# Gated linear attention with a max-out layer: a new opening, eight items transposed on TensorE, and three loads issued from ScalarE's queue

## The chip, the cores and the metric

The kernel runs on one core of a Trainium2 chip. The core has five engines with queues of their own: TensorE (PE in the profile; its weight loads are the row PEld), VectorE (DVE), ScalarE (ACT), GpSimd (POOL) and SyncE (SP), which here only issues transfers. Sixteen DMA engines move data between the device memory and the core. The metric is the device time of one execution in microseconds. The profile's span, from the first to the last instruction, is a little shorter than that time: 168.3 us of span stand beside 170.57 us for the profiled execution.

## What is computed

The inputs q, k, v and alpha have the shape 4 batches x 8 heads x 768 tokens x 48, in float32. A state of 48x48 for each batch and head decays and is updated token by token, and its product with q is the input of a max-out layer:

```
state = alpha[t][:, None] * state + outer(k[t], v[t])
y[t]  = q[t] @ state                      # for each batch and head
x     = y, heads side by side             # 3072 tokens x 384
h1    = x @ w1 ; h2 = x @ w2              # 384 x 1024 each
out   = maximum(h1, h2) @ w_out           # 1024 x 384
```

## The kernel before

**The attention.** The work is cut into 12 items: item n is one batch and 256 tokens of it, three items to a batch, laid out as 128 partitions with two tokens (index j) in each. Lines 403 to 685 (`attention(n)`) plan one item. ScalarE takes the logarithm of alpha (`ln`), VectorE adds pairs of it (`su`), and TensorE turns that into running sums with a triangular matrix (`cs`, lines 435 to 443). ScalarE takes two exponentials of the sums (`en`, `ep`) and one of the few decay factors (`gg`). GpSimd multiplies k by `en` (`kt`, line 474), VectorE multiplies q by `ep` (`qt`, line 480), GpSimd casts v (`vc`, line 489). Both products must be turned so that the head dimension lies on partitions. Items 0 to 4 (the tuple `TURN`, line 194) do it on TensorE against an identity matrix (line 510, 16 products an item) followed by two copies out of PSUM (`ck`, `cq`, line 338 on ScalarE or 340 on VectorE); items 5 to 11 do it by two DMA transposes (line 522). Then come the scores (`sc`, line 620), their mask (`pt`, line 628), the state (`kv`, line 540; `w`, `t32` and `T`, lines 575 to 600, the only chain from one item to the next) and the output `y` (line 674), which is cast into `xT` (`xe`).

**The max-out layer.** Since maximum(h1, h2) = relu(h1 - h2) + h2, the kernel computes relu(x @ (w1 - w2)) @ w_out + x @ (w2 @ w_out). The difference `wd16` (line 375) and the product `m16` (transposes at line 360, products at line 392) are made once from the weights. After that a `group` of tokens needs eight h products of three matmuls each (line 701), eight relus (709 on VectorE, 711 on ScalarE), and for every 128 tokens three matmuls with `m16` (726) and eight with `wo16` (728), an eviction and a store (736). The groups are 2, 3, 3, 3, 3, 3, 3, 2 and 2 blocks of 128 tokens wide.

**What sets the order.** The order on every engine is written out ahead of time. `Plan` (lines 29 to 165) is a list scheduler that runs when the program is built: every operation has estimated durations on the engines that may run it, dependencies, buffers and a priority (smaller first). `run` steps through an estimated clock, gives each idle engine the ready operation of the smallest priority, and emits the instructions in the order in which they started there. On the chip every engine takes its instructions in that fixed order; if an operand comes later than the estimate said, the engine waits, even where other work behind it would be ready. Attention has the priority 100 n plus a small number; the groups have 3000 and more, so they always come behind the attention. A load costs 1.31 us of the plan's transfer time, a DMA transpose 1.15 us. All transfers, transposes and stores are issued by SP, in one order: item 0, then w2, w1 and w_out in quarters (line 323), then items 1 to 11.

**The start.** GpSimd makes the constant matrices (`setup_pool1`) and then clears the pads of the v and T tiles (lines 262 and 276). VectorE derives others from them (`setup_dve1`, `setup_dve2`, lines 250 to 272), and item 0's `su` comes after these on VectorE.

Of the kernel before, what the change touches and what calls it, by code (L numbers as in the profile page):

```python
# [24 lines left out]
class Op:  # L25
    __slots__ = ("name", "engs", "emit", "deps", "takes", "uses", "prio", "mode", "xfer", "eng", "start", "end", "seen", "n")


class Plan:
# [4 lines left out]
    LEAD = 3.0  # L34

    def __init__(self, pools):
        self.free = dict(pools)
        self.banks = [True] * 8
        self.ops = []

    def room(self, takes):
        need = {}
        for b in takes:
            need[b.pool] = need.get(b.pool, 0) + 1
        for p, k in need.items():
            if p == "A":
                if self.pair() is None:
                    return False
            elif p == "M":
                if not any(self.banks):  # L50
                    return False
            elif self.free[p] < k:
                return False
        return True
# [7 lines left out]
    def take(self, b):  # L62
# [3 lines left out]
        elif b.pool == "M":  # L66
            free = [i for i in range(7, -1, -1) if self.banks[i]]
            half = [i for i in free if not self.banks[i ^ 1]]
            b.at = (half or free)[0]
            self.banks[b.at] = False  # L70
        else:
            self.free[b.pool] -= 1

    def give(self, b):
        if b.pool == "A":
            self.banks[b.at] = self.banks[b.at + 1] = True
        elif b.pool == "M":
            self.banks[b.at] = True
        else:
            self.free[b.pool] += 1  # L80

    def add(self, name, engs, emit, deps=(), takes=(), uses=(), prio=0.0, mode=None, xfer=0.0):
        o = Op()
        o.name, o.engs, o.emit, o.prio, o.mode, o.xfer = name, engs, emit, prio, mode, xfer
# [10 lines left out]
    def run(self):  # L95
        idle = {e: 0.0 for e in self.LAT}
        mode = None
        dma = 0.0
        order = []
# [3 lines left out]
        while waiting:  # L103
# [9 lines left out]
            for o in waiting:  # L113
# [6 lines left out]
                if ready is None:  # L120
# [6 lines left out]
                for e, dur in o.engs.items():  # L127
# [6 lines left out]
                    key = (o.prio, o.n)  # L134
                    if e not in best or key < best[e][0]:
                        best[e] = (key, o, dur)
            done = set()
            for e, (key, o, dur) in sorted(best.items(), key=lambda x: x[1][0]):
# [5 lines left out]
                if e == "PE" and o.mode != mode:  # L144
                    dur += self.SWITCH
                    mode = o.mode
# [3 lines left out]
                if e == "SP":  # L150
                    dma = max(dma, t + 1.3) + o.xfer
# [17 lines left out]
def kernel(  # L169
# [23 lines left out]
    WMAX = 384  # L193
    TURN = (0, 1, 2, 3, 4)
# [3 lines left out]
    NLD = 20  # L198
# [14 lines left out]
    plan = Plan({"ld": NLD, "en": 2, "loga": 2, "qk": 3, "pt": 4, "w": 4, "t32": 3, "gg": 3, "g": 2, "g16": 3, "outs": 6})  # L213
# [24 lines left out]
    def setup_pool1(eng):  # L238
        make_upper_triangular(nc, u16, val=1.0, diag=True)
        nc.gpsimd.memset(half1, 0.0)  # L240
# [7 lines left out]
        make_identity(nc, ident16)  # L248

    def setup_dve1(eng):  # L250
        nc.vector.memset(s16s[0][:, :, D:64], 0.0)
        nc.vector.memset(s16s[1][:, :, D:64], 0.0)
        nc.vector.tensor_sub(out=cmat, in0=u16, in1=half1)
        nc.vector.memset(cmat[0:64, 64:128], 0.0)
        nc.vector.tensor_sub(out=us16, in0=u16, in1=ident16)
        nc.vector.tensor_scalar_mul(out=nid16, in0=ident16, scalar1=-1.0)
        for i in range(2):
            nc.vector.memset(qkts[i].rearrange("p a j h d -> p (a j h) d")[:, :, D:64], 0.0)

    def setup_pool2(eng):  # L260
        for t in v16s:
            nc.gpsimd.memset(t.rearrange("p j h d -> p (j h) d")[:, :, D:96], 0.0)

    def setup_dve2(eng):
# [7 lines left out]
        nc.vector.memset(qkts[2].rearrange("p a j h d -> p (a j h) d")[:, :, D:64], 0.0)  # L272

    def setup_pool3(eng):
        for t in T16s:
            nc.gpsimd.memset(t, 0.0)

    s_p1 = plan.add("setp1", {"POOL": 2.6}, setup_pool1, prio=-100)
    s_d1 = plan.add("setd1", {"DVE": 2.6}, setup_dve1, deps=[s_p1], prio=-100)
    s_p2 = plan.add("setp2", {"POOL": 1.6}, setup_pool2, deps=[s_p1], prio=-90)  # L280
    s_d2 = plan.add("setd2", {"DVE": 1.3}, setup_dve2, deps=[s_d1], prio=-80)
    s_p3 = plan.add("setp3", {"POOL": 1.5}, setup_pool3, deps=[s_p2], prio=80)


    LX = 1024 * 20.5 / 16e3
    ld = {}

    def add_load(n, which, prio):
        src = {"a": alpha, "q": q, "k": k, "v": v}[which]
        b, c = divmod(n, NDB)  # L290
        buf = Buf("ld")

        def emit(eng):
            t = A["ld", n, which] = ldp.tile([128, H, 2 * D], FP32, tag="ld", name=which + "f")
            nc.sync.dma_start(  # L295
                out=t, in_=src[b, :, c * 256 : (c + 1) * 256, :].rearrange("h (p j) d -> p h (j d)", j=2)
            )

        ld[n, which] = (plan.add(f"ld{which}{n}", {"SP": 0.65}, emit, takes=[buf], prio=prio, xfer=LX), buf)

    WX = 384 * 1024 / 400e3
    wl = {}

    def add_wload(name, i, prio):
# [3 lines left out]
        def emit(eng):  # L308
            if name == "wo":
                t = ldp.tile([128, 2, DM], FP32, tag="ld", name="wof")  # L310
                nc.sync.dma_start(
                    out=t, in_=src[i * 256 : (i + 1) * 256, :].rearrange("(s p) d -> p s d", p=128)
                )
            else:
                t = ldp.tile([128, 3, 256], FP32, tag="ld", name=name + "f")
                nc.sync.dma_start(
                    out=t, in_=src.rearrange("(s p) f -> p s f", p=128)[:, :, i * 256 : (i + 1) * 256]
                )
            A["w", name, i] = t

        wl[name, i] = (plan.add(f"ld{name}{i}", {"SP": 0.5}, emit, takes=[buf], prio=prio, xfer=WX), buf)

    seq = [("d", 0)] + [("w2", i) for i in range(4)] + [("w1", i) for i in range(4)] + [("wo", i) for i in range(4)]
    seq += [("d", n) for n in range(1, ND)]
    pos = 0
    for name, i in seq:
        if name == "d":
            for w in "aqkv":
                add_load(i, w, -1000 + pos)
                pos += 1  # L330
        else:
            add_wload(name, i, -1000 + pos)
# [11 lines left out]
    w2c, wdc, woc, ptc = [], [], [], []  # L344
    for i in range(4):
        o, b = wl["w2", i]
        w2c.append(plan.add(
            f"w2c{i}", {"ACT": 0.83, "DVE": 0.55, "POOL": 1.25},
            lambda eng, i=i: cast(eng, w216[:, :, i * 256 : (i + 1) * 256], A["w", "w2", i]),
            deps=[o], uses=[b], prio=50 + i))  # L350

    for i in range(4):
        ps = Buf("M")

        def emit(eng, i=i, ps=ps):
            tp = A["wtp", i] = bank(ps, 384).bitcast(FP16).rearrange("p (u m) -> p u m", u=6)
            for u in range(2):
                for s in range(3):
                    f = 2 * i + u
                    nc.tensor.transpose(tp[:, 3 * u + s, :], w216[:, s, f * 128 : (f + 1) * 128], ident16)  # L360

        tr = plan.add(f"wtp{i}", {"PE": 0.34}, emit, deps=[w2c[i], s_p1], takes=[ps], prio=60 + i, mode=0)
        ptc.append(plan.add(
            f"wtc{i}", {"DVE": 0.6, "ACT": 0.8},
            lambda eng, i=i: cast(eng, w2T[:, 2 * i : 2 * i + 2, :].rearrange("p u m -> p (u m)"),
                                  A["wtp", i].rearrange("p u m -> p (u m)")),
            deps=[tr], uses=[ps], prio=61 + i))

    for i in range(4):
        o1, b1 = wl["w1", i]  # L370
        o2, b2 = wl["w2", i]

        def emit(eng, i=i):
            e = nc.vector if eng == "DVE" else nc.gpsimd
            e.tensor_sub(out=wd16[:, :, i * 256 : (i + 1) * 256], in0=A["w", "w1", i], in1=A["w", "w2", i])

        wdc.append(plan.add(f"wd{i}", {"DVE": 1.0, "POOL": 1.9}, emit, deps=[o1, o2], uses=[b1, b2], prio=70 + i))
    for i in range(4):
        o, b = wl["wo", i]
        woc.append(plan.add(  # L380
            f"woc{i}", {"ACT": 0.83, "DVE": 0.55, "POOL": 1.25},
            lambda eng, i=i: cast(eng, wo16[:, 2 * i : 2 * i + 2, :], A["w", "wo", i]),
            deps=[o], uses=[b], prio=74 + i))

    mc = []
    for s in range(3):
        ps = Buf("M")

        def emit(eng, s=s, ps=ps):
            mp = A["mp", s] = bank(ps, DM)  # L390
            for f in range(NF):
                nc.tensor.matmul(mp, lhsT=w2T[:, f, s * 128 : (s + 1) * 128], rhs=wo16[:, f, :],  # L392
                                 start=(f == 0), stop=(f == NF - 1))

        mm = plan.add(f"mp{s}", {"PE": 1.3}, emit, deps=ptc + woc, takes=[ps], prio=78 + s, mode=0)
        mc.append(plan.add(f"mc{s}", {"ACT": 0.48, "DVE": 0.5},
                           lambda eng, s=s: cast(eng, m16[:, s, :], A["mp", s]), deps=[mm], uses=[ps], prio=79 + s))
# [5 lines left out]
    def attention(n):  # L403
# [10 lines left out]
        loga_b = Buf("loga")  # L414

        def e_ln(eng):
            t = A["loga", n] = wk.tile([128, H, 2, D], FP16, tag="loga", name="loga")
# [367 lines left out]
```

## Time and profile before

| | |
|---|---|
| time, three runs | 171.43 us (169.94 to 171.87) |
| span of the profiled execution | 168.3 us |
| TensorE busy | 134.8 us (80%), 2144 matmuls |
| VectorE, ScalarE, GpSimd busy | 77.8, 84.1, 71.5 us |
| first matmul starts, last one ends | 8.47 us, about 164.9 us |
| read from and written to device memory | 23.59 and 4.72 MB |

The page gives the busy time of each engine, then the span in 40 slices of 4.2 us with one digit of busy share each, then the chain of work that ended last, and the groups of instructions by line. A busy TensorE is not a TensorE at its best: the ends of its matmuls are modelled, and at a lower clock the same matmuls are busy longer. So it takes two readings, how long it was idle and how long the same instruction took in different stretches.

### The profile page before, as it was taken

How to read it: one execution, taken by the hardware profiler on the slowest of the kernel's cores; microseconds unless marked ns; L12 is line 12 of the kernel's file. 1: busy time of each engine (PE TensorE's matmuls, PEld its weight loads, DVE VectorE, ACT ScalarE, POOL GpSimd, SP SyncE). 2: the span in 40 equal slices, each digit the busy share in tenths (PEclk: the TensorE clock that was granted, in tenths of full speed). 3: DMA queues.
4: the chain of work that ended last, by engine and by line, in shares of the span. 5: the costliest groups of instructions: out<-in, count | busy, mean ns of one | idle time of the engine just before them, and what ended most of it. 6: DMA issues, size and time to landing. Idle time of an engine off the chain costs nothing.

```text
span 168.3 us, 5032 instructions
## 1 busy us (share of the span) xinstructions
PE 134.8 (80%) x2144; PEld 89.6 (53%) x2144; DVE 77.8 (46%) x136; ACT 84.1 (50%) x155; POOL 71.5 (42%) x113
## 2 busy tenths in 40 slices
PE   0058599967884868969599894789989999999991
PEld 0047466745673645636256672545645666667660
DVE  3939922849678856618269564651930000001100
ACT  3255657453836549533563365262145482926342
POOL 7647900959794696781706467094100000000000
PEclk9999999999999699999879999699999999999999
DMA  5999999999999999999999999967210212103112
GB/s 142 265 346 348 370 280 238 274 247 266 310 241 277 251 257 247 197 268 246 200 237 208 235 254 219 263 78 156 90 51 0 93 47 76 68 25 117 47 47 93
DMA packets 72469, 32.29 MB, mean 192 GB/s; under 512 B 65280, under 2 KB 72448, under 8 KB 72448
## 3 DMA queue, kind: packets, MB, share of 16 engines
q1 hardware_dynamic: 72448, 31.99, 81.7%
q8 instruction: 16, 0.26, 0.7%
q14 instruction: 5, 0.04, 0.1%
HBM read 23.59 MB, written 4.72 MB: 168 GB/s over the span
## 4 chain that ended last, share of the span: by engine, by line
PE 49%; DMA 26%; DVE 7%; POOL 5%; SPq 4%; issue 4%; ACT 3%; DVEq 0%; ACTq 0%; POOLq 0%
PE PS L701 13%; PE PS L728 13%; DMA af<-in_alpha_dram 11%; DMA qk<-qkt 8%; PE PS L674 6%; PE PS L726 5%; DMA vf<-in_v_dram 4%; DMA w2f<-in_moe_w_dram 3%; PE PS L392 3%; SPq L295 3%; DVE pt L628 2%; PE PS L620 2%; POOL qkt L474 2%; PE PS L435 2%; PE PS L510 1%
## 5 line engine op out<-in xcount | busy, mean ns | idle before, releaser
L701 PE MATMUL PS<-xT,wd 128*128 128x384 f16 (+1 forms) x216 | 37.6, 319 | 3.9 <-ACT xT L338 2.6
L728 PE MATMUL PS<-wo,g 128*128 128x384 f16 x192 | 37.2, 326 | 0.0
L628 DVE TENSOR_TENSOR pt<-PS,mask 128x1024 f16<-128x1024 f32 x24 | 28.1, 1217 | 3.8 <-PE PS L620 3.5
L701 PEld LDWEIGHTS <-wd 128*128 128x128 f16 x216 | 20.3, 99 | 15.8 <-issue 4.7
L474 POOL TENSOR_TENSOR qkt<-kf,en 128x768 f16<-128x768 f32 x12 | 21.7, 1813 | 14.9 <-ACT gg L460 6.9
L711 ACT ACTIVATE g<-PS 128x384 f16<-128x384 f32 (+1 forms) x55 | 24.5, 458 | 6.3 <-PE PS L701 5.9
L709 DVE TENSOR_SCALAR g<-PS 128x384 f16<-128x384 f32 (+1 forms) x17 | 7.8, 493 | 37.8 <-PE PS L701 37.1
L338 ACT COPY outs<-PS 128x384 f32<-128x384 f32 x23 | 11.0, 478 | 28.2 <-PE PS L728 28.2
L728 PEld LDWEIGHTS <-g 128*128 128x128 f16 x192 | 18.1, 98 | 11.8 <-ACT g L711 0.2
L418 ACT ACTIVATE loga<-af 128x768 f16<-128x768 f32 x12 | 10.1, 843 | 18.8 <-DMA af<-in_alpha_dram 18.8
L620 PE MATMUL PS<-qk 48*64 48x128 f16 x384 | 9.5, 233 | 9.6 <-DMA qk<-qkt 5.1
L435 PE MATMUL PS<-s,cmat 128*128 128x384 f16 x24 | 8.4, 385 | 9.2 <-DVE s L425 8.5
L726 PE MATMUL PS<-m,xT 128*128 128x384 f16 x72 | 15.7, 326 | 0.0
L489 POOL CAST v<-vf 128x768 f16<-128x768 f32 x12 | 9.9, 823 | 13.0 <-DMA vf<-in_v_dram 12.8
L575 POOL TENSOR_TENSOR T<-w,gg 48x192 f16<-48x192 f32 x24 | 12.9, 539 | 4.3 <-DVE w L600 3.4
L620 PEld LDWEIGHTS <-qk 48*64 48x64 f16 x384 | 7.3, 115 | 13.1 <-issue 12.2
L480 DVE TENSOR_TENSOR qkt<-qf,PS 128x384 f16<-128x384 f32 x24 | 12.0, 546 | 4.0 <-DMA qk<-qkt 4.0
L452 ACT ACTIVATE en<-PS 128x768 f32<-128x768 f32 x12 | 9.7, 807 | 8.3 <-PE PS L443 8.1
L674 PE MATMUL PS<-pt,v 64*64 64x128 f16 x576 | 12.0, 233 | 0.1
L338 ACT CAST xT<-PS 128x384 f16<-128x384 f32 x13 | 7.6, 585 | 7.5 <-PE PS L701 4.5
L340 DVE CAST xT<-PS 128x384 f16<-128x384 f32 x11 | 6.5, 588 | 10.2 <-PE PS L701 5.4
L674 PEld LDWEIGHTS <-v 64*64 64x64 f16 x576 | 9.7, 116 | 1.6 <-issue 0.6
(66 smaller groups left out, 162.1 us busy)
## 6 DMA issues: line engine op xcount, KB each, us to landing
af<-in_alpha_dram SPq DMA_DIRECT2D x12, 384.0 KB, 6.1
qf<-in_q_dram SPq DMA_DIRECT2D x12, 384.0 KB, 5.8
kf<-in_k_dram SPq DMA_DIRECT2D x12, 384.0 KB, 5.7
vf<-in_v_dram SPq DMA_DIRECT2D x12, 384.0 KB, 6.0
out_dram<-outs SPq DMA_DIRECT2D x24, 192.0 KB, 1.9
w2f<-in_moe_w_dram SPq DMA_DIRECT2D x4, 384.0 KB, 5.9
w1f<-in_moe_w_dram SPq DMA_DIRECT2D x4, 384.0 KB, 7.8
wof<-in_moe_w_out_dram SPq DMA_DIRECT2D x4, 384.0 KB, 8.0
```

Source lines behind the costliest of these rows:

```text
L338: nc.scalar.copy(out=out, in_=in_)
L435: nc.tensor.matmul(t[:, g, 0:384], lhsT=cmat, rhs=s16[:, 4 * g : 4 * g + 4, 0:D].unsqueeze(2).to_broadcast([128, 4, 2, D]), start=True, st ...
L474: e.tensor_mul(out=hjd(qkts[i3], 1), in0=A["ld", n, "k"].rearrange("p h (j d) -> p h j d", j=2), in1=A["en", n].rearrange("p g (h j d) -> ...
L480: nc.vector.tensor_mul(out=hjd(qkts[i3], 0)[:, 4 * g : 4 * g + 4], in0=A["ld", n, "q"].rearrange("p h (j d) -> p h j d", j=2)[:, 4 * g : 4 ...
L575: e.tensor_mul(out=T16s[m % 4][o : o + 48, :, 48 * u : 48 * u + 48], in0=w_[o : o + 48], in1=g_[o : o + 48])
L620: nc.tensor.matmul(t[64 * x : 64 * x + 64, u, c0 : c0 + 128].rearrange("p (j m) -> p j m", j=2), lhsT=qk[o : o + D, 1, j, r, 64 * x : 64 * ...
L628: nc.vector.tensor_mul(out=t.rearrange("p u r c -> p (u r) c"), in0=A["sc", n, hf].rearrange("p u (r c) -> p (u r) c", r=2), in1=mask.rear ...
L674: nc.tensor.matmul(dst, lhsT=lhsT, rhs=rhs, start=(x, u) not in begun, stop=ends[x, u] == i, skip_group_check=True)
L701: nc.tensor.matmul(t[:, 0:W], lhsT=wd16[:, s, f * 128 : (f + 1) * 128], rhs=xT[:, s, a0 : a0 + W], start=(s == 0), stop=(s == 2))
L711: nc.scalar.activation(out=o, in_=i, func=ACTF.Relu)
L726: nc.tensor.matmul(A["op", t0], lhsT=xT[:, s, t0 : t0 + 128], rhs=m16[:, s, :], start=(s == 0), stop=False)
L728: nc.tensor.matmul(A["op", t0], lhsT=A["g16", g][:, f, i * 128 : (i + 1) * 128], rhs=wo16[:, f, :], start=False, stop=(f == NF - 1))
```

## The change

The change rewrites the opening and the order.

- **Loads.** alpha of items 0 and 1 comes in two halves of four heads, and k is loaded right after alpha. The weights come in halves instead of quarters: the first halves of w2, w_out and w1 after item 0, the second halves after item 1. q and v of item 0 and the first half of w2 are issued by ScalarE's queue.
- **Items 0 and 1** are worked in two halves of four heads from `ln` to the turned copies, with `kt` on VectorE instead of GpSimd.
- **Weights.** w2 @ w_out is made in two halves: the first is kept in float32 (`m32`), the second is added to it.
- **Transposes.** Items 0 to 7 are turned on TensorE, items 8 to 11 by DMA.
- **Setup.** The clears of the pads move from GpSimd to VectorE, and the mask is made later.
- **Order.** Groups are all two blocks (256 tokens) wide. A group's priority is that of the item three later (`LAG`) instead of coming after all attention, so groups and later items take turns. The plan follows which buffer of a ring is next, [...] lets SP run 4.5 instead of 3.0 us ahead of the transfers, and costs a load at 1.63 us and a DMA transpose at 1.6 us.
- `FILL`, `SHIFT` and `STAY` are empty or zero and do nothing here.

```
+TURN = (0, 1, 2, 3, 4, 5, 6, 7)
+SPLIT = (0, 1)
+LOADS = (0, ("w2", 0), ("wo", 0), ("w1", 0), 1, ("w2", 1), ("wo", 1), ("w1", 1), 2, 3, 4, 5, 6, 7, 8, 9, 10, 11)
+GROUPS = (2,) * 12
+LAG = 3.0
+ONACT = (("q", 0), ("v", 0), ("w2", 0))
+FILL = (0, 0.0)
+SHIFT = {}
...
-    LEAD = 3.0
+    LEAD = 4.5
+    WARM = 4.0
...
+                    if not warm:
+                        recent = [r for r in recent if r[1] > t - self.WARM]
+                        if sum(r[1] - max(r[0], t - self.WARM) for r in recent) > 0.9 * self.WARM:
+                            warm = True
+                        else:
+                            dur *= 2
...
-    TURN = (0, 1, 2, 3, 4)
...
-    NLD = 20
+    NLD = 10
...
-        for i in range(2):
-            nc.vector.memset(qkts[i].rearrange("p a j h d -> p (a j h) d")[:, :, D:64], 0.0)
-
-    def setup_pool2(eng):
-        for t in v16s:
-            nc.gpsimd.memset(t.rearrange("p j h d -> p (j h) d")[:, :, D:96], 0.0)
...
+    def setup_pads(i):
+        nc.vector.memset(qkts[i].rearrange("p a j h d -> p (a j h) d")[:, :, D:64], 0.0)
+        nc.vector.memset(v16s[i].rearrange("p j h d -> p (j h) d")[:, :, D:96], 0.0)
...
-    def setup_pool3(eng):
-        for t in T16s:
-            nc.gpsimd.memset(t, 0.0)
...
-    LX = 1024 * 20.5 / 16e3
+    LX = 1024 * 25.5 / 16e3
...
+    def issue(eng):
+        return nc.scalar if eng == "ACT" else nc.sync
+
+    def on(key):
+        return "ACT" if key in ONACT else "SP"
...
+        hs = [(0, 4), (4, 8)] if n in SPLIT and which == "a" else [(0, 8)]
...
+                issue(eng).dma_start(out=A["ld", n, which][:, h0:h1, :], in_=view[:, h0:h1, :])
...
-    seq = [("d", 0)] + [("w2", i) for i in range(4)] + [("w1", i) for i in range(4)] + [("wo", i) for i in range(4)]
-    seq += [("d", n) for n in range(1, ND)]
...
+            def e_mc(eng, i=i, s=s):
+                if i == 0:
+                    cast(eng, m32[:, s, :], A["mp", s])
+                else:
+                    nc.vector.tensor_add(out=m16[:, s, :], in0=A["mp", s], in1=m32[:, s, :])
...
+        split = n in SPLIT
+        parts = [(0, 4), (4, 8)] if split else [(0, 8)]
...
+            ke = {"DVE": 0.1 + 0.82 * F} if split else {"POOL": 0.1 + 1.72 * F}
...
-            ck = plan.add(f"dk{n}", {"SP": 1.2}, lambda eng: e_tr(eng, 1), deps=[kt], takes=[qkb], prio=-2000 + P, xfer=1.15)
-            cq = plan.add(f"dq{n}", {"SP": 1.2}, lambda eng: e_tr(eng, 0), deps=[qt, ck], uses=[qkb], prio=-2000 + P, xfer=1.15)
...
+            cks.append(plan.add(f"dk{n}", {"SP": 1.2}, lambda eng: e_tr(eng, 1), deps=kts, takes=[qkb], prio=-2000 + P, xfer=1.6))
+            cqs.append(plan.add(f"dq{n}", {"SP": 1.2}, lambda eng: e_tr(eng, 0), deps=[qt, cks[0]], uses=[qkb], prio=-2000 + P, xfer=1.6))
...
-        P = 3000 + 100 * g
+        P = 100.0 * ((c0 + nch - 1) // 2 + LAG)
...
-            plan.add(f"st{g}.{i}", {"SP": 0.65}, e_st, deps=[ev], uses=[ob], prio=-1500 + g, xfer=0.52)
+            plan.add(f"st{g}.{i}", {"SP": 0.65}, e_st, deps=[ev], uses=[ob], prio=-100 + g, xfer=0.52)
...
-    for g, nch in enumerate((2, 3, 3, 3, 3, 3, 3, 2, 2)):
+    for g, nch in enumerate(GROUPS):
```

## The prediction

> **What bounds the kernel now.** I read the page's slices first, then busy time by stretch, then the waits of TensorE and of the transfer queue, then the opening in order of time.
>
> Three rows of the page's slices: transfers are near full up to slice 27 (about 113 us), TensorE is full only after that, and its clock dips three times.
>
> ```profile
> PE   0058599967884868969599894789989999999991
> PEclk9999999999999699999879999699999999999999
> DMA  5999999999999999999999999967210212103112
> ```
>
> TensorE by stretch (columns: stretch, length, then busy time of PE, PEld, DVE, ACT, POOL with counts, granted clock, transfer share, GB/s):
>
> ```profile
> 28.00:40.00 12.00, 9.65 (x149) 6.78 (x149) 8.04 (x18) 6.31 (x12) 8.59 (x12) 1.00 1.09 259
> ...
> 50.00:60.00 10.00, 6.62 (x175) 4.77 (x173) 8.11 (x13) 5.69 (x9) 6.30 (x11) 0.83 1.10 257
> ...
> 80.00:90.00 10.00, 7.93 (x104) 4.42 (x108) 5.32 (x7) 5.31 (x10) 3.28 (x7) 0.83 1.11 228
> ...
> 100.00:110.00 10.00, 6.88 (x95) 3.85 (x95) 6.20 (x10) 4.02 (x8) 4.91 (x7) 0.84 1.26 233
> ...
> 130.00:160.00 30.00, 30.00 (x198) 19.17 (x197) 0.85 (x2) 16.16 (x37) 0.00 (x0) 1.00 0.19 67
> ```
>
> From 130 us TensorE never waits; between 28 and 130 us it is idle for 17.4 us, while VectorE, ScalarE and GpSimd are each under 90% busy. No engine bounds that stretch: TensorE waits in a fixed order on late operands with max-out work queued behind. The waits, longest total first (columns: waiter, releaser, total us, times, longest):
>
> ```profile
> PE PS L620 <- DMA qk<-qkt: 5.1, 3, 3.1
> PE PS L701 <- ACT xT L338: 2.6, 2, 2.1
> PE PS L540 <- ACT xT L338: 2.2, 2, 1.2
> ...
> SPq L522 <- POOL T L575: 7.7, 3, 3.2
> SPq L522 <- DVE qkt L480: 4.0, 2, 2.7
> SPq L522 <- DVE w L600: 3.1, 2, 1.8
> ```
>
> The first line is scores waiting for DMA transposes. The SPq lines are those transposes waiting for compute at the head of the one transfer queue, with later loads behind them.
>
> Last, the opening, on VectorE and then on TensorE (start, length):
>
> ```profile
> 3.21 0.22 DVE L255 TENSOR_TENSOR us<-u,ident 128x128 f16<-128x128 f16 x1 [0.96 <-POOL ident masks.py:199]
> 3.35 3.78 DVE L256 TENSOR_SCALAR nid<-ident 128x128 f16<-128x128 f16 x1
> ...
> 8.05 0.36 DVE L425 TENSOR_TENSOR s<-loga 128x384 f16<-128x384 f16 x1
> ...
> 22.54 5.19 PE L392 MATMUL PS<-wo,w2T 128*128 128x384 f16 x24
> ```
>
> A 128x128 operation takes 3.78 us while GpSimd clears memory (3.12 to 7.08 us); `loga`, done at 5.20 us, is summed only at 8.05. The first max-out matmul comes at 28.16 us, after all weights.
>
> [...] line 392 takes 5.12 us / 24 = 0.213 us each in the chain, later 384-column matmuls 0.162, and the dips to 0.83 stand where TensorE is idle for 2 to 3 us. [...]
>
> **TensorE's work at full clock.** From the chain: three 384-column matmuls 0.49 us (0.1625 each), 24 of 256 columns 2.73 us (0.11 each, three 0.33). One item: sums 0.56 (0.16+0.08+0.16+0.08+0.08), state 0.37, scores 0.57, output 1.36: 2.86 us. Transposes of an item on TensorE: two of 0.44 us (33.38 to 33.82 us), so 0.88.
> - Before: h 144 x 0.1625 + 72 x 0.11 = 31.3; line 728 31.2; line 726 11.7; attention 12 x 2.86 = 34.3; transposes 5 x 0.88 = 4.4; weights 24 x 0.054 (128 columns at the same rate) + 24 x 0.1625 = 5.2. Sum 118.
> - By 28.2 us about 9.3 of this is done (item 0 with its transposes 3.7, the weights 5.2, item 1's sums 0.5). The last 108.8 us are done between 28.2 and 164.9, in 136.7 us. So 27.9 us are lost: 17.4 idle and 10.5 to the slow clock and ends of bursts. This is what the change can win.
>
> **The change part by part.**
> - *Setup.* With the clears off GpSimd, `nid` should take under 0.4 us. VectorE gets four T clears and six pad clears, at 0.1 to 0.5 us (VectorE clears of before 0.11 to 0.27, GpSimd's 0.53 and 0.74), about 2 us, part of it before alpha lands. `su` can start near 5, and with half an alpha near 4.5: TensorE starts 3 to 4 us earlier[...].
> - *Three loads on ScalarE.* Issues took 0.46 to 1.24 us each on SP. On ScalarE three cost 1.5 to 3.5 us between its table load (ending 2.01) and the first `ln` (4.36 before). Behind them wait `ln`, `su` and the sums. At most 1 us, [...] I take 0.5 us of loss, inside the 3 to 4 gained.
> - *Weights in halves, item 1 between them.* Bytes stay; loads are the bound here (share 1.1). By 28 us TensorE can have done items 0 and 1 (7.5), half of the weights (2.6), and half the h products of two groups (2 x 4 x 0.33 = 2.7): 12.8 instead of 9.3. The float32 half adds three evictions of about 0.5 us beside other work.
> - *Three more items on TensorE:* 3 x 0.88 = 2.6 us more of TensorE. Six copies, 0.68 us on VectorE (line 340) or 1.02 on ScalarE, together 4 to 6 us on engines that are 46 and 50% busy: hidden in sum, a latency of about 1.5 us per item, but against 4.3 us (median) for a DMA transpose. Six transposes leave the transfers. Between 60 and 110 us 11 of them, 18 loads and 6 stores share 50 us; 18 x 1.39 (four loads issued from 24.80 to 30.36) = 25 and 6 x 0.6 = 3.6 leave at most 1.9 us each, waits included, so 6 give back up to 11 us. Groups that finish earlier put some 6 stores (3.6 us) into the same stretch.
> - *Groups of two:* 96 x 0.33 = 31.7 against 31.3 us, +0.4. Relus become 96 of about 0.39 us (256 columns: 0.38 and 0.42) against 32.2 us in all: +5 us on the two engines, beside TensorE.
> - *Lag of three, truer costs.* Older groups get TensorE before newer attention, so an item's casts and transposes have a group of 6.2 us ahead of them. Loads issued 1.39 us apart were planned at 1.31, with transposes too cheap; now both are costed above the pace seen, and late operands in the fixed order should be fewer. I price this only as a share of the 27.9 us.
>
> TensorE's work after is 118 + 2.6 + 0.4 = 121; 108.2 remain at 28.2 us, as many as before: the opening's gain pays for the transposes. The end is 28.2 + 108.2 + L + 3.4 (164.9 to the span's end before) = 139.8 + L, and the time is 2.5 us more (2.3 in the profiled execution, 3.1 against the median): 142.3 + L. So all hangs on L, which was 27.9.
>
> Half should go: 5.1 us on transposes mostly (none before item 8), part of the 8 us on `xT` and casts, and [...] the clock dips, some 5 us. I take L = 14: 156 us. Transfers don't bind: item 11's last load, issued at 103.4 us before, comes some 7 us earlier, near 97; its output was cast 23 us later (126.4), so near 120, and a group and the tail follow, near 130.
>
> **The rivals.**
> - *TensorE nearly dense*, L = 4 to 8: 146 to 150 us. For it: the 30 us after 130 with no wait. Against: scores, masks (1.22 us, twice an item) and the T chain on GpSimd stay serial.
> - *The waits move.* Scores wait for `ck` and `cq` instead of DMA, copies queue behind relus, and the fixed order stalls as often; L = 20 to 27 gives 162 to 169, L = 28 gives 170 (no change). For it: the waits on `xT` are also waits for those engines.
> - *Slower.* More instructions per item on VectorE (copies, `kt`, clears), mid-stretch at 8.1 of 10 busy already (50 to 60 us), make it the pacemaker; groups that compete with attention delay the last items, and stores hold loads back. L = 34: 176 us. Against: VectorE is 46% busy overall.
>
> **How the numbers follow.** L near 14 (152 to 162 us): 0.53, so 156. Dense (under 152): 0.20. Waits partly moved (162 to 169.7): 0.13; no change: 0.05. Slower: 0.09. Faster 0.86, same 0.05, slower 0.09. From 146 to 169.5 leaves out about 0.05 below and 0.14 above.
>
> **What would show it.** `nid` under 0.5 us and a first matmul near 5 us; a first max-out matmul before 20 us; transposes 8 in number; TensorE's idle time between 28 and its end near 8 us and no clock under 0.9 there; busy TensorE some 135 us or less. Wrong if VectorE or ScalarE stands at 9 tenths through the middle, if scores wait for copies, or if transfers stay full to 113 us and TensorE starves.

## The result, and the profile after

The changed kernel takes 157.25 us (156.95 to 157.53, four runs) beside 171.35 us for the kernel before (169.94 to 171.87): a ratio of 0.919, with a 95% interval of 0.913 to 0.925. The prediction was 156.0. The span went from 168.3 to 155.7 us. Some executions of a kernel were slower at a lower granted clock (in one case below 162.95 us at 0.956 beside 158.49 us at 1.00); the ratios and intervals leave these out, the times and their ranges keep them.

The slices of the changed kernel's page, 3.9 us each:

```profile
PE   0205988769999989997998988999989999999991
PEclk9999999999999999999999999999999999999999
DMA  4999999999999999999999930755388238202202
```

TensorE is nearly full from slice 10 (35 us) on, the three dips of its clock are gone, and the transfers are near full up to slice 23 (90 us) instead of 26 (109 us; slice 27, which the prediction named, shows 6 tenths). The second slice of 2 tenths, followed by a zero, is new: TensorE starts at 5.2 us, has two short bursts, and then nothing to do from 8.2 until 12.9.

Busy time by stretch of the changed kernel, columns as in the prediction (stretch, length, busy PE, PEld, DVE, ACT, POOL, clock, transfer share, GB/s):

```profile
8.00:12.00 4.00, 0.17 (x3) 0.08 (x1) 0.88 (x2) 1.03 (x3) 0.95 (x2) 1.00 1.05 364
...
28.00:40.00 12.00, 9.92 (x156) 6.49 (x154) 9.13 (x15) 5.29 (x12) 6.68 (x9) 1.00 1.15 261
...
50.00:60.00 10.00, 9.36 (x253) 7.45 (x251) 8.83 (x18) 7.36 (x14) 7.39 (x10) 1.00 1.14 258
...
80.00:90.00 10.00, 9.43 (x175) 6.54 (x166) 7.18 (x14) 4.25 (x8) 5.44 (x9) 1.00 1.12 291
...
100.00:110.00 10.00, 10.00 (x132) 6.84 (x131) 4.79 (x12) 4.93 (x10) 4.11 (x6) 1.00 0.61 168
```

From 28 us to TensorE's last matmul (152.4 us) it is idle for 6.8 us, against 17.4 before (to 164.8). "Idle time after 28 us" below is always this: TensorE's, from 28 us to its last matmul. VectorE is busy for 8.8 of 10 us between 50 and 60 us (8.1 before), and for 96.5 us in all (77.8 before).

The order of the transfer queue changed more than the prediction saw. These are SP's issues around the last load (start, length):

```profile
83.15 1.38 SPq L358 DMA_DIRECT2D ldf<-in_v_dram  x1
84.59 4.09 SPq L822 DMA_DIRECT2D out_dram<-outs  x6
97.37 1.34 SPq L606 DMA_TRANSPOSE qk<-qkt  x1
```

The last load is issued at 83.15 us (103.37 before), the first store after it, the first DMA transpose after that: the 40 loads of items 2 to 11 run with nothing between them.

The wait that the experiments point to lay on ScalarE. Its longest waits after 28 us, first the kernel before, then the changed one (waiter, releaser, total us, times, longest):

```profile
ACT outs L338 <- PE PS L728: 28.2, 22, 3.4
ACT loga L418 <- DMA af<-in_alpha_dram: 15.0, 10, 3.4
ACT en L452 <- PE PS L443: 8.1, 5, 4.0
```

```profile
ACT outs L398 <- PE PS L814: 17.1, 17, 2.7
ACT g L797 <- PE PS L787: 16.1, 23, 3.3
ACT xT L398 <- PE PS L760: 12.0, 5, 3.2
```

Before, ScalarE stood for 15.0 us with the logarithm at the head of its queue, waiting for alpha to land. In the changed kernel that line is absent after 28 us; what ScalarE waits for is TensorE. How 15 us on a half-idle engine reach TensorE is seen in two short views of the kernel before, ScalarE and then TensorE:

```profile
46.55 0.80 ACT L456 ACTIVATE PS<-PS 128x768 f32<-128x768 f32 x1
50.00 0.84 ACT L418 ACTIVATE loga<-af 128x768 f16<-128x768 f32 x1 [2.66 <-DMA af<-in_alpha_dram]
50.75 0.57 ACT L338 CAST xT<-PS 128x384 f16<-128x384 f32 x1
```

```profile
50.12 0.30 PE L540 MATMUL PS<-v,qkt 64*64 64x48 f16 x2
51.37 0.43 PE L540 MATMUL PS<-v,qkt 64*64 64x48 f16 x30 [0.96 <-ACT xT L338]
```

The cast of `xT` comes behind the logarithm, so it starts only when alpha has landed and the logarithm is nearly through; the state product waits for that cast, and all max-out work behind it on TensorE waits too.

How much of the time hung on such landings is seen in the chain of work that ended last. After 40 us, the chain of the kernel before runs through these transfers (start, length):

```profile
42.96 6.96 DMA af<-in_alpha_dram
...
62.00 6.75 DMA af<-in_alpha_dram
...
76.14 5.28 DMA af<-in_alpha_dram
...
87.96 7.05 DMA qk<-qkt
...
100.26 5.76 DMA qk<-qkt
```

It goes three times through a landing of alpha (19.0 us, the transfers' own time included), and then twice through a DMA transpose (12.8 us). In the changed kernel's chain neither stands after 28 us.

### The profile page after: what moved, and what is told of

Read it like the earlier page. It is cut to its first block, busy times and chain, and to the rows that moved or that the text cites. A ratio compares the mean times of both kernels' runs of the same rounds, so it can differ in the third digit from the quotient of the medians.

```text
span 155.7 us, 5328 instructions
## 1 busy us (share of the span) xinstructions
PE 132.3 (85%) x2264; PEld 93.8 (60%) x2264; DVE 96.5 (62%) x193; ACT 78.4 (50%) x160; POOL 64.2 (41%) x106
## 4 chain that ended last, share of the span: by engine, by line
PE 72%; DVE 8%; DMA 7%; ACT 5%; POOL 3%; issue 3%; ACTq 0%; DVEq 0%
PE PS L814 20%; PE PS L787 20%; PE PS L760 9%; PE PS L812 8%; DMA ldf<-in_moe_w_dram 7%; PE PS L585 4%; PE PS L706 4%; PE PS L626 2%; DVE pt L714 2%; PE PS L521 2%; PE PS L446 2%; DVE xT L400 2%; DVE wd L436 1%; POOL qkt L559 1%; ACT xT L398 1%
## 5 line engine op out<-in xcount | busy, mean ns | idle before, releaser
L787 PE MATMUL PS<-xT,wd 128*128 128x256 f16 x288 | 38.8, 273 | 4.9 <-DVE xT L400 1.7
L559 POOL TENSOR_TENSOR qkt<-ldf,en 128x768 f16<-128x768 f32 x10 | 18.1, 1815 | 26.7 <-issue 15.0
L795 DVE TENSOR_SCALAR g<-PS 128x256 f16<-128x256 f32 x43 | 17.6, 421 | 18.0 <-PE PS L787 17.4
L797 ACT ACTIVATE g<-PS 128x256 f16<-128x256 f32 x53 | 19.6, 384 | 16.5 <-PE PS L787 16.1
L398 ACT CAST xT<-PS 128x384 f16<-128x384 f32 x12 | 7.1, 592 | 17.0 <-PE PS L760 13.3
L565 DVE TENSOR_TENSOR qkt<-ldf,PS 128x384 f16<-128x384 f32 x24 | 12.3, 548 | 2.6 <-ACT gg L548 1.6
L575 POOL CAST v<-ldf 128x768 f16<-128x768 f32 (+1 forms) x14 | 10.2, 734 | 6.5 <-DMA ldf<-in_v_dram 5.9
L585 PE MATMUL PS<-ident,qkt 128*128 128x128 f16 x128 | 11.2, 231 | 1.8 <-DVE qkt L565 0.6
L539 ACT ACTIVATE en<-PS 128x768 f32<-128x768 f32 (+1 forms) x14 | 10.0, 721 | 5.0 <-PE PS L529 4.8
L502 ACT ACTIVATE loga<-ldf 128x768 f16<-128x768 f32 (+1 forms) x14 | 10.4, 749 | 2.5 <-DMA ldf<-in_alpha_dram 2.5
L585 PEld LDWEIGHTS <-qkt 128*128 128x128 f16 x128 | 8.7, 103 | 3.7 <-issue 1.0
```

Of the source, the lines that this page charges most:

```text
L398: nc.scalar.copy(out=out, in_=in_)
L559: e.tensor_mul(out=hjd(qkts[i3], 1)[:, hd], in0=A["ld", n, "k"][:, hd].rearrange("p h (j d) -> p h j d", j=2), in1=A["en", n][:, g0:g1].re ...
L565: nc.vector.tensor_mul(out=hjd(qkts[i3], 0)[:, 4 * g : 4 * g + 4], in0=A["ld", n, "q"].rearrange("p h (j d) -> p h j d", j=2)[:, 4 * g : 4 ...
L585: nc.tensor.transpose(A["tp", n][:, a, r, j, :], src[:, j, r, :], ident16)
L787: nc.tensor.matmul(t[:, 0:W], lhsT=wd16[:, s, f * 128 : (f + 1) * 128], rhs=xT[:, s, a0 : a0 + W], start=(s == 0), stop=(s == 2))
L795: nc.vector.tensor_relu(o, i)
```

## The experiments

Two theories stood at the start: DMA transposes among the loads starved TensorE (theory 1), or the order of the work did, by its priorities or by the plan's costs (theory 2; for the runs built on the kernel before it is called theory 3). Theories 4 and 5 came with the last four runs. The times of the kernel before on the same chips were 171.4 to 171.8 us in all comparisons (medians). An edit of a constant of the plan changes the order of the whole program, so differences of a few us between two plans are not the edit's own price: w2's place, tried in two orders, won 6.4 us in one and lost 5 in the other (the last run).

### Items 5 to 7 back to DMA transposes

```
-TURN = (0, 1, 2, 3, 4, 5, 6, 7)
+TURN = (0, 1, 2, 3, 4)
```

> The changed kernel with only items 0 to 4 turned on TensorE, so items 5 to 7 again go through DMA transposes. Theory 1 (transfers): in the kernel before, DMA transposes waiting at the head of the one transfer queue held the loads back (last load issued at 103 us, now at 83) and starved TensorE; then the last load is again issued after 95 us and the time is 163 to 170 us, with TensorE idle over 12 us after 28 us. Theory 2 (order: groups that take turns with attention, and truer plan costs, keep TensorE supplied): TensorE has a backlog of max-out work, the loads come later but nobody waits, and the time stays at 155 to 159 us.

158.69 us (158.15 to 162.95), ratio 0.934 (0.913 to 0.955). As theory 2 expected: the transposes are back among the loads, the first issued at 60 us, and it costs 1.4 us. The last load comes at 102 us, as late as theory 1 said, but TensorE doesn't starve: its idle time after 28 us is 9.9 us.

### Groups after all attention, as before

```
-        P = 100.0 * ((c0 + nch - 1) // 2 + LAG)
+        P = 3000 + 100 * g
```

> The changed kernel with the groups' priority of before (3000 and more: after all attention). Theory 2 (order): attention is again placed just in time, the fixed order stalls on late casts and masks, TensorE is idle 12 us or more after 28 us and the time is 163 to 170 us. Theory 1 (transfers): the priority is not what mattered, idle time stays near 7 us and the time at 155 to 160 us.

153.25 us (153.01 to 154.16), ratio 0.904 (0.894 to 0.914): faster than the changed kernel by 4.0 us, which neither theory expected. Idle time after 28 us is 2.9 instead of 6.8 us, and that difference is most of the gain. With these costs in the plan the new priority isn't what helped.

### The first half of w2 back on SP's queue

```
-ONACT = (("q", 0), ("v", 0), ("w2", 0))
+ONACT = (("q", 0), ("v", 0))
```

> The changed kernel with the first half of w2 issued by SP, ahead of w_out and w1, and only q and v of item 0 on ScalarE's queue. In the changed kernel w2 was issued at 1.96 us and was cast only at 12.39 us, and item 0's k product waited behind that cast on VectorE. Theory A (transfers of two queues share the engines, so w2 on the second queue is slowed by w_out and w1 on the first): in one queue w2 lands near 9 us, the first weight transposes start by 10 us instead of 12.9, and the time falls by 1.5 to 3 us to 154 to 156. Theory B (12.4 us is what the bytes ahead cost in any order): w2 is cast after 11.5 us and the time stays within 1 us of 157.2.

150.90 us (150.43 to 152.11), ratio 0.890 (0.879 to 0.902), the fastest of all, and faster than either theory said. VectorE in the opening, first the changed kernel, then this run:

```profile
12.39 0.76 DVE L400 CAST w<-ldf 128x512 f16<-128x512 f32 x2 [2.54 <-DMA ldf<-in_moe_w_dram]
13.52 0.85 DVE L400 COPY w2T<-PS 128x512 f16<-128x512 f16 x2 [0.37 <-PE PS L420]
14.29 1.02 DVE L559 TENSOR_TENSOR qkt<-ldf,en 128x384 f16<-128x384 f32 x2
```

```profile
9.39 1.02 DVE L559 TENSOR_TENSOR qkt<-ldf,en 128x384 f16<-128x384 f32 x2
10.65 0.42 DVE L400 COPY qk<-PS 128x512 f16<-128x512 f16 x1 [0.23 <-PE PS L585]
11.13 0.76 DVE L400 CAST w<-ldf 128x512 f16<-128x512 f32 x2
```

The transfer itself lies between theories A and B: 768 KB land 8.8 us after their issue in place of 10.4, and are cast at 11.13 instead of 12.39. In the first 16 us the packets of SP's and ScalarE's queues took 63.3 and 35.3% of the time of the 16 DMA engines in the changed kernel, and 77.1 and 21.2% here. Item 0's k is held up too: issued at 1.80 us, it lands 9.4 us later in the changed kernel, and 7.3 us later here. These landings are measured; that the sharing of the engines is their cause isn't shown alone. The larger part is order: with w2 on ScalarE's queue the plan puts the cast of w2 ahead of item 0's k product, which then waits for w2 until 14.29 us though k is there at 11.2. With w2 on SP the product runs at 9.39, and item 0's scores start at 12.92 instead of 18.66. Up to 28 us this saves 1.5 us of idle time; the other 5 us lie later, in a different order of the whole, with 3.4 us of idle time after 28, and are not explained further.

### All loads on SP's queue

```
-ONACT = (("q", 0), ("v", 0), ("w2", 0))
+ONACT = ()
```

> The changed kernel with all loads on SP's queue. If the second queue saves issue time that counts, alpha and k are not later but v and w2 are, and the time rises by 1 to 2 us (158 to 159). If it mainly makes the first transfers share the engines, the time falls to 154 to 156, close to the run with only w2 moved.

152.81 us (151.90 to 154.06), ratio 0.901 (0.887 to 0.915): 4.4 us faster than the changed kernel, a larger fall than either reading named. The second queue's earlier issue (w2 at 1.96 us in the changed kernel, at 4.53 here) doesn't show as time won. Its clock is told of at the end.

### The kernel before with eight items on TensorE, and nothing else

```
-    TURN = (0, 1, 2, 3, 4)
+    TURN = (0, 1, 2, 3, 4, 5, 6, 7)
```

> The kernel before with items 0 to 7 turned on TensorE, nothing else changed. Theory 1 (transfers: DMA transposes among the loads starved the middle): the last load is issued before 95 us instead of 103, TensorE's idle time between 28 and 130 us falls from 17.4 to under 10 us, the time to 160 to 165 us. Theory 3 (the middle is lost to a plan that is wrong about durations and buffers, and to a slow clock in the opening): TensorE's idle time stays above 14 us, and the time is 169 to 174 us.

169.54 us (168.63 to 171.70), ratio 0.992 (0.986 to 0.997). The transfers are relieved as theory 1 wants it (the last load is issued at 91 us), and 1.9 us come of it. Idle time after 28 us is 12.3 us (theory 1 had named under 10, theory 3 over 14), and TensorE's clock in that stretch is 0.94 (0.96 before). The wait for alpha is longer than ever:

```profile
ACT loga L418 <- DMA af<-in_alpha_dram: 19.2, 7, 4.3
```

Theory 3's time is right. Theory 1's gain of 6 us or more doesn't come, though TensorE's own wait for DMA transposes falls from 5.1 to 0.5 us.

### The same with truer transfer costs in the plan

```
-    LEAD = 3.0
+    LEAD = 4.5
...
-    LX = 1024 * 20.5 / 16e3
+    LX = 1024 * 25.5 / 16e3
```

and 1.6 for 1.15 us as the cost of a DMA transpose.

> The kernel before with items 0 to 7 turned on TensorE and the plan's truer transfer costs (a load 1.63 us, a DMA transpose 1.6 us, SP 4.5 us ahead). If the costs are what removes the stalls, this is at least 3 us faster than the run with the transposes alone, 157 to 165 us. If they are not, both are within 1.5 us of each other, and what is left to the change is its opening and its model of buffers.

153.61 us (152.80 to 154.14), ratio 0.898 (0.893 to 0.903): 16 us less than the run above, by three constants that only the plan reads, and below the range that was named. After 28 us no wait for alpha is left, and TensorE is idle for 3.6 us.

### The changed kernel with the old costs

The same three constants set back, and the plan's first TensorE durations no longer doubled (`dur *= 2` in the diff).

> The changed kernel with the plan's costs of before: a load 1.31 us, a DMA transpose 1.15 us, SP 3.0 us ahead, and TensorE taken at full clock from the start. If truer costs are what keeps TensorE supplied, its idle time after 28 us rises from 6.8 to over 12 us and the time to 162 to 168 us. If not, the time stays at 154 to 160 us.

156.28 us (155.07 to 157.09), ratio 0.913 (0.906 to 0.921). The costs that are worth 16 us in one kernel are worth nothing in the other. Idle time after 28 us is 6.2 us, ScalarE's wait for alpha 1.8 us. So something else in the changed kernel protects it.

### The changed kernel with the old count of buffers

```
-            elif not all(self.free[p][(self.turn[p] + i) % len(self.free[p])] for i in range(k)):
+            elif sum(self.free[p]) < k:
...
-            b.at = self.turn[b.pool]
+            b.at = self.free[b.pool].index(True)
```

> The changed kernel with the plan counting free buffers of a ring as before, instead of following which one is next. On the chip buffers are still taken in turn, so the plan believes in buffers that are not free yet. If that was a source of the stalls before, TensorE idles over 12 us after 28 us and the time is 161 to 168 us. If the rings rarely run dry, the time stays at 155 to 159 us.

156.90 us (156.42 to 157.54), ratio 0.917 (0.913 to 0.922): no difference: following which buffer is next isn't what helped.

### The kernel before with truer costs alone

The three constants as above, items 0 to 4 on TensorE as before.

> The kernel before, items 0 to 4 on TensorE as before, with only the plan's transfer costs changed (load 1.63 us, DMA transpose 1.6 us, SP 4.5 us ahead). Theory 4 (late alpha: the plan places ScalarE's logarithm of alpha before alpha has landed, and the casts of xT queue behind it): ScalarE's wait for alpha after 28 us falls from 15.0 to under 5 us and the time to 153 to 160 us, although all 14 DMA transposes stay. Theory 1 (transfers): with the transposes still among the loads the time stays above 164 us.

154.41 us (153.70 to 155.49), ratio 0.902 (0.896 to 0.908), with the transposes among the loads, the old opening and the old priority. ScalarE's longest waits after 28 us:

```profile
ACT outs L338 <- PE PS L728: 21.2, 19, 2.4
ACT xT L338 <- PE PS L674: 12.8, 8, 2.6
ACT g L711 <- PE PS L701: 3.9, 9, 1.4
```

Alpha is gone from the list (15.0 us before), and TensorE's idle time after 28 us falls from 17.4 to 6.2 us. The view of ScalarE shows one place: the logarithm runs without a wait, and the cast of `xT` right behind it.

```profile
45.23 0.84 ACT L418 ACTIVATE loga<-af 128x768 f16<-128x768 f32 x1
46.04 0.59 ACT L338 CAST xT<-PS 128x384 f16<-128x384 f32 x1
```

Two rivals can be read from the same trace. GpSimd's wait for v after 28 us stays (11.0 us before, 9.2 here), so late v can't be most of what cost the time. TensorE's wait for DMA transposes fell with the rest (5.1 to 0.7 us); but the run with eight items on TensorE takes that wait away by itself, and gains 1.9 us.

### Eight items on TensorE and only the load's cost

> The kernel before with items 0 to 7 on TensorE and only the cost of a load in the plan raised from 1.31 to 1.63 us. Theory 4 puts the whole gain of 16 us on this number: 153 to 157 us, ScalarE's wait for alpha after 28 us under 4 us (19.2 without it). If the transposes' cost or SP's lead matter as much, it is 158 to 166 us.

160.08 us (159.84 to 161.19), ratio 0.936 (0.930 to 0.941): the time lies in the range of the second reading, not of theory 4. The load's cost alone gives 9.5 us of the 16, and the wait for alpha after 28 us falls from 19.2 to 0.7 us. So with the wait for alpha gone two fifths of the loss were still there: that wait isn't the whole of it. The other 6.5 us are the transposes' cost and SP's lead; which of them wasn't tried. Idle time after 28 us is 8.4 us.

### The changed kernel with the old priority and the old costs

> The changed kernel with both the groups' priority of before (after all attention) and the plan's old costs. With the new costs the old priority took 153.3 us; with the new priority the old costs took 156.3. Theory 5 (the new priority is a second cure for the same thing: groups ahead of attention leave slack, so late alpha hurts nobody): with neither cure the stalls return, 161 to 168 us, and ScalarE waits for alpha over 8 us after 28 us. If it stays at 152 to 157 us, the stores' place behind the loads or the new opening is what made the changed kernel insensitive to the costs.

166.68 us (165.93 to 167.39), ratio 0.971 (0.964 to 0.978). The stalls are back: 13.1 us idle after 28 us, a clock of 0.66 between 80 and 90 us, and this line, just under the 8 us that theory 5 named:

```profile
ACT loga L502 <- DMA ldf<-in_alpha_dram: 7.9, 5, 3.4
```

The four runs make a square:

| changed kernel with | costs above the real pace | old costs |
|---|---|---|
| groups in turn with attention | 157.25 us | 156.28 us |
| groups after all attention | 153.25 us | 166.68 us |

Either cure removes the stalls. Without the higher costs the lag is worth 10 us. With them it shows a loss of 4 us, which is within what another order can do: with w2 on SP's queue as well, the lag is worth 7.4 (the next run).

### Both edits that were faster

w2 on SP and groups after all attention.

> The changed kernel with the first half of w2 on SP's queue and groups after all attention, the two edits that each made it faster (by 6.4 and 4.0 us). If the gains add (opening and steady middle are separate stretches), 146 to 148 us; if both only filled the same idle time, 150 to 152 us.

158.30 us (156.34 to 158.77), ratio 0.917 (0.908 to 0.926). The two gains of 6.4 and 4.0 us don't add; together they are slower than either, and outside both ranges that were named. Why stays open. It is a different order of 5,300 instructions, and the gains of single edits were partly that too. The fastest version measured is the changed kernel with w2 on SP.

## Why the prediction was right or wrong

*The number and its frame: right.* All was put on the loss L beside TensorE's work, with L = 14 against 27.9 before. From the span of 155.7 us and the prediction's formula L was 15.9. TensorE's work by 28 us was 9.6 us, not 12.8 (item 0 3.6, item 1's sums, state product and three quarters of its transposes 1.6, weights 1.1 + 2.0, twelve h matmuls 1.3). So 111.4 us remained and were done by 152.45 us: 12.8 us lost after 28.2, and 3.2 in the opening. The half was right, in part by luck, as the reasons given for it were not the ones found. Idle time after 28 us was 6.8 where about 8 was named, the clock never fell under 0.9 there (1.00 in its mean), busy TensorE was 132.3 us where 135 or less was named, and eight DMA transposes remained.

*Why the half goes: wrong, and this is the step that failed.* "5.1 us on transposes mostly" took the longest wait in TensorE's own list. Undoing the three items' transposes costs 1.4 us, doing them alone brings 1.9. What held TensorE was a plan that took transfers too short; its largest sign is ScalarE waiting for alpha, ahead of the casts that TensorE needed. That the costs did it is shown three times, by 17.3, 15.9 and 13.4 us (in the kernel before, in it with eight items on TensorE, and in the changed kernel with groups last, there together with the plan's doubling of TensorE's first durations). That the way led through alpha is read from the waits and the chain, not shown alone: no run moved only the logarithm, and one such wait of 3.5 us stands in the fastest run too. The prediction counted "part of the 8 us on `xT` and casts" but didn't ask what those casts stood behind. The page had the lines: `loga` idle 18.8 us before alpha, and in the chain alpha with 11% of the span, DMA transposes with 8%.

*Lag and truer costs: the price was left as a share, and the two were not told apart.* Truer costs alone bring 17.3 us in the kernel before (154.41 against 171.71), more than the whole change. "Loads issued 1.39 us apart were planned at 1.31" was the right observation with no price on it. The lag, named as a help, is a clear help only where the costs are too low.

*Three loads on ScalarE: mis-sized.* The issue time was right (0.47 + 0.65 + 1.84 = 2.96 us, within 1.5 to 3.5), and the first `ln` wasn't later (4.30 us against 4.36). The 0.5 us of loss was the author's estimate, and it didn't show: item 0's first sum starts on VectorE at 4.86 us, and at 4.83 with q on SP's queue behind alpha. The item that hurt was w2: on its own queue it landed 1.3 us later than on SP's, k landed 2.1 us later, and the plan put w2's cast ahead of item 0's k product. Moving w2 back gains 6.4 us in this order, of which 1.5 us are seen in the opening. The prediction had priced the issues and the work that waits behind them, but not that w2 would land later on the second queue (10.4 us after its issue there, 8.8 on SP's). For the same reason "a first max-out matmul before 20 us" failed: it came at 24.21, and with w2 on SP's queue it comes at 19.35.

*Setup: right.* `nid` takes 0.18 us instead of 3.78, with nothing running on GpSimd from 3.08 to 8.46 us, and the first sums start on TensorE at 5.17 us, as these lines of the changed kernel show:

```profile
3.47 0.18 DVE L298 TENSOR_SCALAR nid<-ident 128x128 f16<-128x128 f16 x1
...
4.86 0.26 DVE L510 TENSOR_TENSOR s<-loga 128x192 f16<-128x192 f16 x1 [0.93 <-ACT loga L502]
...
5.17 0.48 PE L521 MATMUL PS<-s,cmat 128*128 128x384 f16 x1 [5.17 <-DVE s L510]
```

That GpSimd's clears had held `nid` up is read from the overlap (3.12 to 7.08 us), not shown alone. But the 3 us won were lost again: TensorE waited for w2 until 12.9 us.

*Transfers: right that they don't bind, wrong in size.* The last load was to be issued near 97 us and was at 83, because nothing came between the loads. Six stores had been counted there: the change gave stores a priority behind all loads, and the diff shows it (-1500 + g became -100 + g); six were issued together from 84.6 us on. The remaining DMA transposes, which the sum left in that stretch, came after 97 us as well.

*The rival "the waits move"* was right in kind only: TensorE still waits for masks, copies and casts after 28 us, but for none of them longer than 0.7 us at a time.

*A sign of being wrong that wasn't one:* "VectorE or ScalarE stands at 9 tenths through the middle". VectorE does so in slices 15 to 17 (54 to 66 us), and TensorE is at 8 and 9 tenths there.

*The clock: read too simply.* The prediction saw the dips "where TensorE is idle for 2 to 3 us". That fits the waits of 2.07 us (to 82.81, with a clock of 0.50 from 84 to 86 us) and 3.12 us (to 106.06, 0.50 from 108 to 110). The dip between 54.7 and 58.9 us (0.60) has no such wait before it: from 48 to 54.7 us TensorE is busy for 3.92 of 6.7 us, with waits of 0.19 to 0.96 us. What sets the clock isn't shown by these runs.

Not tried alone: the new setup, groups of two, the split of items 0 and 1, the weights in halves, the store's priority.

## What to carry to other kernels

Where the order on every engine is fixed ahead of time, a duration that the plan takes too small can stall an engine with all that is queued behind it. Here loads that came every 1.39 us did harm when planned at 1.31 us in three of the four kernels where this was tried, and none that showed at 1.63; larger values weren't tried. So check each planned transfer against the pace in the trace, and try the upper side. To find where such a stall begins, don't stop at the wait on the engine that limits the time; follow it back to what its releaser had waited for, and look at what the chain runs through. And undo the parts of a large change one at a time and in pairs: here two cures hid each other. A single undoing says little where it reorders everything: w2's second queue cost 6 us in one order and won 5 in another.

## What the runs showed of the hardware

In the opening TensorE ran at half its pace without the clock row saying so. In the changed kernel's chain four 384-column matmuls take 1.28 us, 0.32 each, twice the 0.163 of the three later ones, in a stretch whose granted clock reads 1.00:

```profile
17.03 1.28 PE PS L446 x4
...
35.61 0.49 PE PS L812 x3
```

The opening of the kernel before shows it too: from the start of line 435's second matmul of 384 columns to that of the next matmul it is 0.32 us at 8.90 us and 0.16 us at 27.81, and the clock reads 1.00 in both stretches.

And while it was busy, TensorE stayed near half clock for 12 us. With all loads on SP's queue, these stretches follow each other:

```profile
24.00:28.00 4.00, 3.24 (x80) 2.67 (x80) 3.37 (x7) 1.97 (x4) 2.65 (x7) 0.59 1.06 382
28.00:32.00 4.00, 3.64 (x69) 2.48 (x68) 2.67 (x5) 1.89 (x4) 2.40 (x3) 0.50 1.00 237
32.00:36.00 4.00, 4.00 (x20) 2.37 (x19) 1.94 (x4) 1.46 (x4) 1.05 (x1) 0.63 1.06 248
```

TensorE is 81 to 100% busy and its clock is 0.50 to 0.63. Its twelve 384-column matmuls of line 446 take 4.02 us in this time (from 31.07 us on), 0.335 each. No idle gap from TensorE's start in this run (4.2 us) to the end of these stretches is over 1 us long; the longest are 0.98 us (to 23.29) and 0.90 us (to 6.71). This run has the least idle time up to 28 us of the changed kernel's variants (9.9 us, against 13.3 in the changed kernel and 11.9 with w2 on SP), and didn't turn it into the shortest time; twelve matmuls of line 446 that take 4.02 us here are busy for 2.16 us with w2 on SP (from 27.53 us on, at a clock of 1.00), so part of this lower idle time is no gain.
